# Attention with a soft mixture of experts: the products with v cut by halves of the queries, the last keys on four parts of TensorE

## The chip, the cores and the metric

One core of a Trainium2 chip runs the whole program. The metric is the device time in microseconds of one execution; three runs of the kernel before took 546.36, 547.23 and 550.35 us (median 547.23 us).

## The reference

There are 8 batches of 8 heads, 576 queries and keys, head dimension 64. What is computed, cut to what matters:

```python
scores = (q @ k.T) / 8                       # per batch and head, 576 x 576
attn = exp(scores - max) * (scores >= max - tau)
attn = attn / (sum(attn) + 1e-9)
x = attn @ v                                 # 576 x 64 per head; joined: 4608 tokens x 512
logits = x @ phi                             # 32 slots (8 experts of 4)
slots = softmax_over_tokens(logits).T @ x    # 32 x 512
slots = relu(slots @ w1[e]) @ w2[e]          # 8 experts, 512 x 1024 and 1024 x 512
out = softmax_over_slots(logits) @ slots     # 4608 x 512
```

All of it is in 32-bit floating point. The trace shows two records for each matmul on such numbers and one for each transpose.

## The kernel before

**The loop.** Two heads make a pair; the loop runs over 32 pairs (four per batch), and after each fourth pair `dispatch` (line 953) computes the logits and the running sums of that batch. In `pair` (line 717) the queries of the two heads are cut into nine blocks of 128: eight blocks of 512 "main" queries, and one block (i = 8) with the 64 left queries of both heads. For each block TensorE forms the scores (line 774; line 779 for block 8), VectorE negates them into SBUF and keeps the row maximum (L786), ScalarE takes the exponential (L796), GpSimd makes the threshold (L799), and VectorE masks and sums (L802). TensorE then transposes the masked blocks through `ptr` (line 690; 8 + 8 + 8 + 8 pieces for the main blocks, 2 for the last 64 keys of the first half, 7 for block 8 and the last keys of the second half) and ScalarE copies the transposes out of PSUM: `pTa` and `pTb` (first and second half of the queries, keys 0 to 511) and `pTl` (the 64 last keys; L695, and L874 for two pieces of 64 x 64).

**The products with v** (line 892) are two blocks of work, A (`pTa`, 256 queries) and B (`pTb`, 320 queries: 256 main and the 64 left ones). Each takes five steps over the keys (four of 128 and one of the 64 last keys) for two heads: 10 matmuls, or 20 records. Head h writes columns of the array h*64 to h*64+63, so the two heads run beside each other. The fifth step works over all 128 rows of the array, although only 64 keys are left: for head 0 rows 64 to 127 of v are zeros, for head 1 rows 0 to 63. ScalarE copies each block into `xT`; `xT` is transposed into `x`, GpSimd scales it by the reciprocal of the row sums (`ri`), and it is transposed back (line 916) and copied into `xT` (L919).

**PSUM** is four regions of two banks; each block of scores, each group of transposes and each block of products takes a region until it is copied out.

**The order of the work** is written out: `Order.add` (line 431) records each operation with its engine, a cost and its reads and writes; `TABLE` holds due times by scope (`pair0`, `pair1a`, ..., `batch`) and number; `Order.plan` (line 458) sorts each engine's queue strictly by due time and gives out buffers; `Order.run` emits the work. So the sorted due times are the order in which each engine works.

**After the loop** come the softmax over slots, the experts (`stage1`, `stage2`) and `combine`. 26 pieces of 512 KB of w1 and w2 are loaded during the loop, 20 more (`host`) into SBUF that the loop has given back, and 18 more through tiles already used; all of these loads stand in SP's queue.

**The names used below:** A, B: the two blocks of products. Scores on the array: two row halves at once (lines 774 and 690, 916), two column halves at once (line 892), four quarters at once (line 779), four column strips (lines 974, 1022, 1027: logits and running sums).

Of the kernel before, what the change touches and what calls it, by code (L numbers as in the profile page):

```python
# [17 lines left out]
LAT = {"PE": 252, "DVE": 150, "ACT": 165, "POOL": 86, "SP": 4500}  # L18
CROSS = {("PE", "DVE"): 260, ("DVE", "ACT"): 182, ("DVE", "POOL"): 220, ("ACT", "DVE"): 237, ("ACT", "POOL"): 250,
         ("POOL", "DVE"): 61, ("POOL", "ACT"): 100}  # L20
# [18 lines left out]
for _n, _v in (  # L39
    ("first", [  # L40
# [7 lines left out]
    ]),  # L48
# [8 lines left out]
    ]),  # L57
# [8 lines left out]
    ]),  # L66
# [8 lines left out]
    ]),  # L75
# [8 lines left out]
    ]),  # L84
    ("last", [
# [20 lines left out]
    ("end", [
# [29 lines left out]
    ]),  # L136
# [1260 lines left out]
```

## Time and profile before

| | |
|---|---|
| median of three runs | 547.23 us |
| profiled execution, first to last instruction (its own time) | 545.1 us |
| TensorE busy | 524.6 us, 96% |
| VectorE busy | 473.8 us, 87% |
| ScalarE busy | 459.5 us, 84% |
| GpSimd busy | 234.1 us, 43% |
| one group of four pairs, logits to logits | 57.66 us |
| granted TensorE clock, mean | 0.992 |

The loop takes about 470 of the 545 us. Busy time counts an instruction from its start to its modelled end; instructions that follow each other closely overlap, so the cost of one is better read from the distance of two starts.

### The profile page before, as it was taken

To read this page: it belongs to the slowest core of one execution; us is meant where nothing else is said; L and a number is where in the kernel's file an instruction comes from. 1 tells how busy PE (TensorE), PEld (TensorE's weight loads), DVE (VectorE), ACT (ScalarE), POOL (GpSimd) and SP (SyncE) were. 2 spreads that over 40 slices of the span, in tenths; PEclk is the share of its full clock that TensorE was granted. 3 is DMA by queue.
4 is the path that set the end of the run, shared out by engine and by line. 5 is a ranking of instruction groups with operands and counts; after the bars stand their busy time and mean duration, and the time that the engine had idled before them with its cause. 6 is when DMAs were issued, how large, how long until landed. Compare 5 with 4: busy or idle time off the path is not lost.

```text
span 545.1 us, 18237 instructions
## 1 busy us (share of the span) xinstructions
PE 524.6 (96%) x7016; PEld 339.9 (62%) x7016; DVE 473.8 (87%) x1333; ACT 459.5 (84%) x789; POOL 234.1 (43%) x475
## 2 busy tenths in 40 slices
PE   8999999999999999999999999999999999999990
PEld 6666666666666666666766666666666666644470
DVE  6999999999999999999999999998999999623192
ACT  3999998999899989999999989998999989611181
POOL 2554544554345444553455435554564445021030
PEclk9999999999999999999999999999999999999996
DMA  6433335557472738275424333333334223899598
GB/s 154 92 90 92 96 90 189 162 161 182 118 214 85 215 91 244 60 211 129 130 66 117 90 91 93 91 91 92 83 76 114 52 53 130 334 408 407 207 372 320
DMA packets 31990, 83.03 MB, mean 152 GB/s; under 512 B 4640, under 2 KB 12832, under 8 KB 31904
## 3 DMA queue, kind: packets, MB, share of 16 engines
q1 hardware_dynamic: 31584, 81.43, 49.1%
q8 instruction: 55, 0.90, 0.7%
q10 hardware_dynamic: 320, 0.44, 0.3%
q14 instruction: 31, 0.25, 0.1%
HBM read 72.42 MB, written 9.44 MB: 150 GB/s over the span
## 4 chain that ended last, share of the span: by engine, by line
PE 77%; DVE 7%; ACT 6%; DMA 4%; issue 3%; SPq 0%; DVEq 0%; POOL 0%; POOLq 0%; ACTq 0%
PE ps L892 27%; PE ps L774 22%; PE ps L690 16%; PE ps L779 3%; ACT p L796 2%; PE ps L916 2%; DVE ss L786 2%; DMA host<-in_w 2%; DMA w<-in_w 2%; DVE p L802 2%; PE ps L1022 2%; PE ps L974 2%; PE h L1219 1%; ACT pTa L695 1%; DVE host L1308 1%
## 5 line engine op out<-in xcount | busy, mean ns | idle before, releaser
L786 DVE TENSOR_SCALAR_CACHE_REDUCE ss<-ps 128x576 f32<-128x576 f32 x288 | 208.4, 752 | 12.4 <-issue 3.7
L802 DVE SCALAR_TENSOR_TENSOR p<-ss,thr,p 128x576 f32<-128x576 f32 x256 | 206.4, 836 | 2.3 <-POOL thr L799 1.4
L796 ACT ACTIVATE p<-ss,nmx 128x576 f32<-128x576 f32 x256 | 187.5, 775 | 11.0 <-DVE ss L786 10.0
L799 POOL TENSOR_SCALAR thr<-nmx,pabs 128x1 f32<-128x1 f32 x288 | 121.1, 425 | 158.4 <-DVE ss L786 148.8
L774 PE MATMUL ps<-k,q 64*128 64x288 f32 x1024 | 166.7, 429 | 0.7 <-issue 0.2
L774 PEld LDWEIGHTS ps<-k,q 64*128 64x128 f32 x1024 | 84.5, 189 | 25.9 <-ACT pTb L695 4.8
L690 PEld LDWEIGHTS ps<-ident,p 64*128 64x128 f32 x2304 | 88.9, 138 | 18.1 <-DVE ss L786 2.9
L690 PE MATMUL ps<-ident,p 64*128 64x64 f32 x2304 | 98.0, 223 | 0.4 <-ACT pTl L874 0.2
L695 ACT COPY pTb<-ps 128x1024 f32<-128x1024 f32 (+1 forms) x96 | 83.4, 877 | 2.8 <-PE ps L690 2.1
L892 PE MATMUL ps<-pTb,vv 128*64 128x320 f32 x512 | 76.0, 439 | 0.0
L695 ACT COPY pTa<-ps 128x1024 f32<-128x1024 f32 x64 | 64.9, 1015 | 1.3 <-PE ps L690 1.0
L892 PE MATMUL ps<-pTa,vv 128*64 128x256 f32 x512 | 62.3, 385 | 0.2 <-ACT pTa L695 0.2
L892 PEld LDWEIGHTS ps<-pTb,vv 128*64 128x64 f32 x512 | 33.9, 136 | 32.7 <-issue 3.9
L892 PEld LDWEIGHTS ps<-pTa,vv 128*64 128x64 f32 x512 | 33.9, 136 | 25.2 <-DVE ss L786 6.2
L911 POOL TENSOR_TENSOR x<-x,ri 128x512 f32<-128x512 f32 x31 | 34.8, 1122 | 20.0 <-ACT x L695 19.8
L892 PE MATMUL ps<-pTl,vv 128*64 128x256 f32 (+1 forms) x256 | 41.9, 406 | 0.0
L833 POOL TENSOR_SCALAR pL<-pL,ri 128x576 f32<-128x576 f32 x31 | 24.4, 788 | 27.4 <-DVE ri L829 14.5
L695 ACT COPY xT<-ps 128x256 f32<-128x256 f32 (+1 forms) x62 | 24.7, 401 | 5.3 <-PE ps L892 3.5
L802 DVE SCALAR_TENSOR_TENSOR pL<-ss,thr,pL 128x576 f32<-128x576 f32 x32 | 26.1, 816 | 1.5 <-ACT pL L796 1.4
L892 PEld LDWEIGHTS ps<-pTl,vv 128*64 128x64 f32 x256 | 18.4, 137 | 12.7
L695 ACT COPY pTl<-ps 128x256 f32<-128x256 f32 x64 | 23.9, 374 | 2.5 <-PE ps L690 1.8
L754 POOL TENSOR_SCALAR k<-k,flag 128x576 f32<-128x576 f32 x31 | 24.7, 797 | 2.9 <-DMA k<-in_kT 1.7
(166 smaller groups left out, 532.3 us busy)
## 6 DMA issues: line engine op xcount, KB each, us to landing
w<-in_w SPq DMA_DIRECT2D x44, 512.0 KB, 8.4
q<-in_qT SPq DMA_DIRECT2D x62, 288.0 KB, 4.5
vv<-in_vt SPq DMA_DIRECT2D x32, 320.0 KB, 4.2
host<-in_w SPq DMA_DIRECT2D x20, 512.0 KB, 8.5
k<-in_kT SPq DMA_DIRECT2D x62, 144.0 KB, 3.4
out<-w SPq DMA_DIRECT2D x8, 512.0 KB, 3.4
out<-host SPq DMA_DIRECT2D x8, 512.0 KB, 5.1
out<-host SPq DMA_DIRECT2D x4, 256.0 KB, 4.5
```

The source lines that it names most:

```text
L690: nc.tensor.transpose(out=s[:, g, c:c + 64], in_=ins[g], identity=ident[rows[g], rows[g]], tile_position=(64 * g, 0))
L695: G.add("ACT", 51 + 0.833 * n, nom, lambda: nc.scalar.copy(*io()), r, w)
L754: sc = lambda e, kc=kc: lambda: e.tensor_scalar(out=kt.t[:, kc], in0=kt.t[:, kc], scalar1=flag8, **one)
L774: nc.tensor.matmul(s.t[:, g, 0:HS], qt.t[rows[g], h, c * 128:(c + 1) * 128], kt.t[rows[g], h * HS:(h + 1) * HS], start=True, stop=True, ti ...
L779: nc.tensor.matmul(s.t[rows[a], g, 0:HS], qt.t[rows[g], a, SM:S], kt.t[rows[g], a * HS:(a + 1) * HS], start=True, stop=True, tile_position ...
L786: dve(674, t + OFF['mx'], [s], [ss, nmx], lambda s=s, ss=ss, nmx=nmx: nc.vector.tensor_scalar(out=ss.t.rearrange("p (a k) -> p a k", a=2), ...
L796: G.add("ACT", 668, t + OFF['ex'], lambda sv=sv, nmx=nmx, view=view: nc.scalar.activation(view().rearrange("p (a k) -> p a k", a=2), sv(), ...
L799: pool(250, t + OFF['th'], lambda nmx=nmx, thr=thr: nc.gpsimd.tensor_scalar(out=thr.t, in0=nmx.t, scalar1=1.0, scalar2=pabs, op0=ALU.mult, ...
L802: fn=lambda sv=sv, thr=thr, view=view, i=i: nc.vector.scalar_tensor_tensor(out=view().rearrange("p (a k) -> p a k", a=2), in0=sv(), scalar ...
L833: pool(725, t + OFF['sc'], lambda k=k, view=view_: nc.gpsimd.tensor_scalar(out=view(), in0=view(), scalar1=ri.t[:, k:k + 1], **one), [ri[c ...
L892: nc.tensor.matmul(lone(w)[h * 64:(h + 1) * 64, 0:n], vv.t[:, v0:v0 + 64], p0, start=(kb == 0), stop=(kb == 4), tile_position=(0, h * 64), ...
L911: G.add("POOL", 1040, u + 6.8, own=f"new{j}" + group(b), r=[ri[0]], w=[x[j]], fn=lambda: nc.gpsimd.tensor_tensor(out=wide(), in0=wide(), i ...
```

## The change

1. **Products.** For the first 31 pairs the blocks A and B now hold 256 main queries each, and the two column halves of the array take the two halves of these queries (128 each) instead of the two heads; the heads lie in the two banks of the region. A and B have 16 matmuls of 128 columns each (four steps over the keys, two heads, two halves).
2. **The last 64 keys** of A and B become work of their own, KA and KB: four matmuls of 128 columns on the four quarters of the array (rows by head, columns by half of the queries), added to the sums of A and B.
3. **The left queries** become a block L: 10 matmuls of 64 columns, two heads beside each other as before.
4. **Copies.** `pTl` takes one more third in the copy of block 8 (384 columns) instead of two copies of 64 x 64 (L874). The results are copied as 256, 256 and 64 columns instead of 256 and 320. `pL` gets a border of zeros on both sides, set once before the loop by two memsets on VectorE.
5. **Smaller work.** The reciprocals of a pair (L829, L840) and their GpSimd forerunners (L826, L837) become one each for all nine columns. The maximum of the logits is taken by the operation that also writes them negated to `l4`, so ScalarE's copy of 192 columns goes.
6. **All due times of the loop are new**, those of most pairs apart from each other, and the planner's costs of entering and leaving an arrangement of the array with them. Two of the steps of the softmax over slots (`soft`) are due later than before.
7. The last pair keeps A and B as they were, but its last keys use 64 rows.

TensorE's queue from one batch's logits to the next, sorted by due time (s0 to s8: scores; t0 to t3, tl, pT8: transposes; x, x2: transposes of the result and back; wx, w1: running sums; the number behind the point is the pair). Before, 82 pieces:

```
logits xl s2.14 A.13 dT l4 pT8.13 s0.14 wx w1 t2.13 s7.14 t3.13 s6.14 s8.14 x.12 s5.14 s4.14 t0.14 B.13 x2.12
tl.14 t1.14 s0.15 s1.15 s3.15 t2.14 s2.15 A.14 pT8.14 s6.15 t3.14 s8.15 s4.15 x.13 t0.15 s5.15 s7.15 B.14 x2.13
tl.15 t1.15 s5.16 t2.15 s1.16 s0.16 s3.16 pT8.15 t3.15 s8.16 A.15 s2.16 x.14 s6.16 s7.16 s4.16 t0.16 B.15 x2.14
tl.16 t1.16 s1.17 t2.16 s5.17 s3.17 s0.17 pT8.16 s2.17 A.16 t3.16 s7.17 x.15 s8.17 s6.17 t0.17 s3.18 B.16 s4.17
x2.15 s1.18 t1.17 tl.17
```

After, 94 pieces:

```
logits KA.13 A.13 l4 dT t2.13 s7.14 s0.14 pT8.13 wx w1 t3.13 x.12 s6.14 s4.14 s5.14 t0.14 s8.14 KB.13 L.13 B.13
tl.14 x2.12 t1.14 s0.15 s1.15 s3.15 s6.15 s2.15 t2.14 KA.14 A.14 x.13 pT8.14 s4.15 t3.14 s8.15 KB.14 t0.15 s5.15 s7.15
L.14 B.14 x2.13 t1.15 tl.15 s5.16 t2.15 s1.16 s0.16 s3.16 t3.15 pT8.15 s8.16 KA.15 A.15 x.14 s2.16 s4.16 s6.16 s7.16
t0.16 B.15 L.15 KB.15 x2.14 tl.16 t1.16 s1.17 t2.16 s0.17 s2.17 s3.17 s5.17 s6.17 t3.16 KA.16 A.16 x.15 pT8.16 s7.17
s3.18 t0.17 L.16 B.16 KB.16 s8.17 tl.17 x2.15 s4.17 s2.18 s1.18 t1.17 xl
```

The core of the diff:

```diff
+                            for a in range(2):
+                                nc.tensor.matmul(
+                                    area(w, h, l)[rows[a]], vv.t[:, (h * 4 + kb) * 64:][:, 0:64],
+                                    pT.t[:, h, kb, a * 128:(a + 1) * 128], tile_position=(0, a * 64),
+                                    **flags(w, h, a, l, 5))
+                G.add("PE", 1722, n0, main, [pTa if l == 0 else pTb[2], pTa if l == 0 else pTb[3], vv],
+                      [ab[l]["m", l], xT["t"]], mode=COLS, more=-89)
...
+            def left_keys_product(ls):
+                for l in ls:
+                    for h in range(2):
+                        for a in range(2):
+                            nc.tensor.matmul(
+                                area(ab[l], h, l)[rows[a]], vv.t[rows[h], SM + h * 64:][:, 0:64],
+                                pTl.t[rows[h], (l * 2 + a) * 128:][:, 0:128], tile_position=(64 * h, 64 * a),
+                                **flags(ab[l], h, a, l, 5))
...
                 for kb in range(5):
                     for h in range(2):
-                        v0, p0 = ((h * 4 + kb) * 64, pT.t[:, h, kb, :]) if kb < 4 else (SM + h * 64, pTl.t[:, q])
+                        v0, p0 = ((h * 4 + kb) * 64, pTb.t[:, h, kb, SM - QA:]) if kb < 4 else (
+                            SM + h * 64, pTl.t[:, SM + h * 64:][:, 0:64])
...
+                    G.add("ACT", 264, n0 + OFF['ae'], lambda l=l: nc.scalar.copy(
+                        xT.t[:, l * 256:(l + 1) * 256].rearrange("p (h x) -> p h x", h=2), ab[l].t[:, :, 0:128]),
...
-                for g in range(2):
-                    f = lambda e, w=w, g=g: e(pTl.t[rows[g], SM:S], w.t[rows[1 - g], g, 256:320])
...
+                    act_copy(384, t + OFF['te'], [w], [pTl[2]], lambda w=w: (
+                        pTl.t[:, 256:640].rearrange("p (k g q) -> p k g q", k=3, g=2),
+                        w.t[:, :, 256:448].rearrange("p g (k q) -> p k g q", k=3)))
...
+                dve(90, t + OFF['ri'], [], [ri], lambda: nc.vector.reciprocal(ri.t, ri.t))
...
-        act_copy(192, u + 1.7, [wl], [l4], lambda: (l4.t, lone(wl)[:, 0:192]))
+        G.skip(1)
```

## Rows read from the trace of the kernel before

**Rows 1.** The page, parts 1 and 4: busy time, and the chain by engine.
```profile
PE 524.6 (96%) x7016; PEld 339.9 (62%) x7016; DVE 473.8 (87%) x1333; ACT 459.5 (84%) x789; POOL 234.1 (43%) x475
...
PE 77%; DVE 7%; ACT 6%; DMA 4%; issue 3%; SPq 0%; DVEq 0%; POOL 0%; POOLq 0%; ACTq 0%
```

**Rows 2.** Chain of waits in order of time (start us, us, what), loop and tail.
```profile
2.44 3.77 DMA k<-in_kT
...
202.68 1.46 PE ps L974 x64
...
260.34 1.46 PE ps L974 x64
...
479.34 10.35 DMA host<-in_w
```

**Rows 3.** Busy time by stretches: one group of four pairs, and the loop's end.
```profile
202.68:260.34 57.66, 57.30 (x822) 38.07 (x826) 55.19 (x158) 54.84 (x95) 27.40 (x57) 1.00 0.57 159
440.00:465.00 25.00, 24.15 (x332) 15.21 (x330) 24.28 (x63) 22.97 (x39) 11.68 (x19) 1.00 0.23 77
```

**Rows 4.** TensorE's timeline (start us, us, line, tiles, forms, records), middle of the loop.
```profile
162.85 0.71 PE L774 MATMUL ps<-k,q 64*128 64x288 f32 x4
163.48 1.95 PE L892 MATMUL ps<-pTa,vv 128*64 128x256 f32 x16
...
165.79 0.52 PE L690 MATMUL ps<-ident,pL 64*128 64x64 f32 x10
...
166.28 0.70 PE L774 MATMUL ps<-k,q 64*128 64x288 f32 x4
166.82 0.65 PE L690 MATMUL ps<-ident,p 64*128 64x64 f32 x16
167.83 0.72 PE L779 MATMUL ps<-k,q 64*64 64x288 f32 x8 [0.36 <-ACT pTl L874]
168.48 0.76 PE L774 MATMUL ps<-k,q 64*128 64x288 f32 x4
169.07 0.41 PE L690 MATMUL ps<-ident,xT 64*128 64x64 f32 x8
169.31 0.67 PE L690 MATMUL ps<-ident,p 64*128 64x64 f32 x16
169.81 1.24 PE L774 MATMUL ps<-k,q 64*128 64x288 f32 x8
170.98 2.38 PE L892 MATMUL ps<-pTb,vv 128*64 128x320 f32 x16
...
173.83 0.47 PE L916 MATMUL ps<-ident,x 64*128 64x64 f32 x8
174.13 0.79 PE L690 MATMUL ps<-ident,p 64*128 64x64 f32 x20
```

**Rows 5.** Groups of weight loads: line, form, count, busy us, mean ns, idle before.
```profile
L892 PEld LDWEIGHTS ps<-pTa,vv 128*64 128x64 f32 x512 | 33.9, 136 | 25.2 <-DVE ss L786 6.2 <-ACT p L796 2.3 <-DVE ri L840 1.5
```

**Rows 6.** Groups of VectorE and ScalarE by form: the small work that changes.
```profile
L840 DVE RECIPROCAL ri<-ri 128x8 f32<-128x8 f32 x31 | 6.1, 196 | 0.0
L829 DVE RECIPROCAL ri<-ri 128x1 f32<-128x1 f32 x31 | 4.8, 156 | 1.0 <-POOL ri L826 1.0
...
L695 ACT COPY pTl<-ps 128x256 f32<-128x256 f32 x64 | 23.9, 374 | 2.5 <-PE ps L690 1.8
...
L695 ACT COPY xT<-ps 128x320 f32<-128x320 f32 x31 | 13.2, 426 | 4.1 <-PE ps L892 2.6
L874 ACT COPY pTl<-ps 64x64 f32<-64x64 f32 x62 | 12.8, 207 | 1.0
L695 ACT COPY xT<-ps 128x256 f32<-128x256 f32 x31 | 11.6, 376 | 1.2 <-PE ps L892 0.9
...
L695 ACT COPY l<-ps 128x192 f32<-128x192 f32 x8 | 2.5, 312 | 3.8 <-DVE M L980 3.8
```

**Rows 7.** Waits of SP's queue after 440 us: who, for whom, us, times, longest.
```profile
SPq L672 <- DVE p L802: 11.7, 1, 11.7
```

More of the change, by code (lines that the diff above doesn't have):

```diff
@@ L25 @@
 )
-HALVES, COLS, COLS4, QUADS, WHOLE = range(5)
-SWITCH = 145
+TURN, SCORE, QUADS, COLS, COLS4, WHOLE = range(6)
+ENTER = [
+    [0, 61, 166, 176, 0, 57],
+    [-5, 5, 166, 176, 0, 57],
+    [50, 109, 5, 176, 0, 57],
+    [50, 109, 166, 27, 0, 57],
+    [50, 109, 166, 176, 0, 57],
+    [50, 109, 166, 176, 0, 0],
+]
+LEAVE = [
+    [0, 0, 95, 95, 95, 145],
+    [0, 0, 94, 94, 94, 94],
+    [0, 0, 0, 0, 0, 0],
+    [0, 0, 0, 0, 0, 0],
+    [0, 0, 0, 0, 0, 0],
+    [94, 94, 94, 94, 94, 0],
+]
 PERIOD = 14142.5
 REGIONS = 4
+ONE = False
+QL = ((0,), (1,))
 NPRE = 26
@@ new lines @@
+    ("half0@72", [
+        18564.3, 19183.7, 19171.6, 21768.6, 24815.1,
+    ]),
+    ("half0@108", [
+        17619.3, 18238.7, 18226.6, 20823.6, 23870.1,
+    ]),
+    ("half0@144", [
+        16674.3, 17293.7, 17281.6, 19878.6, 22925.1,
+    ]),
+    ("half0@180", [
+        15729.3, 16348.7, 16336.6, 18933.6, 21980.1,
+    ]),
+    ("new0@36", [
+        36255.1, 38300.4, 43829.8,
+    ]),
+    ("new0@72", [
+        35332.1, 37355.4, 42884.8,
+    ]),
+    ("new0@108", [
+        34387.1, 36410.4, 41939.8,
+    ]),
@@ new lines @@
+    ("new0@144", [
+        33442.1, 35465.4, 40994.8,
+    ]),
+    ("new0@180", [
+        32497.1, 34520.4, 40049.8,
+    ]),
[8 rows of a table added]
+    ]),
[8 rows of a table added]
+    ]),
[8 rows of a table added]
+    ]),
[8 rows of a table added]
+    ]),
[8 rows of a table added]
+    ]),
+    ("half1@45", [
+        11263, 22477, 22477.1, 19848.3, 29943.4,
+    ]),
+    ("half1@81", [
+        10318, 21532, 21532.1, 18432, 28998.4,
+    ]),
+    ("half1@117", [
+        9373, 20587, 20587.1, 17487, 28053.4,
+    ]),
+    ("half1@153", [
+        8428, 19642, 19642.1, 16542, 27108.4,
+    ]),
+    ("half1@189", [
+        7483, 18697, 18697.1, 15597, 26163.4,
+    ]),
@@ new lines @@
+    ("new1@45", [
+        35496.9, 38263.2, 42245.1,
+    ]),
+    ("new1@81", [
+        34551.9, 37318.2, 41300.1,
+    ]),
+    ("new1@117", [
+        33606.9, 36373.2, 40355.1,
+    ]),
+    ("new1@153", [
+        32661.9, 35428.2, 39410.1,
+    ]),
+    ("new1@189", [
+        31716.9, 34483.2, 38465.1,
+    ]),
[8 rows of a table added]
+    ]),
[8 rows of a table added]
+    ]),
[8 rows of a table added]
+    ]),
[8 rows of a table added]
+    ]),
[8 rows of a table added]
+    ]),
+    ("half2@54", [
+        15249.8, 17118, 21254.7, 20558.2, 27906.7,
+    ]),
+    ("half2@90", [
+        14304.8, 16173, 20309.7, 19613.2, 26961.7,
+    ]),
@@ new lines @@
+    ("half2@126", [
+        13359.8, 15228, 19364.7, 18668.2, 26016.7,
+    ]),
+    ("half2@162", [
+        12414.8, 14283, 18419.7, 17723.2, 25071.7,
+    ]),
+    ("half2@198", [
+        11469.8, 13338, 17474.7, 16778.2, 24126.7,
+    ]),
+    ("new2@54", [
+        37182.3, 42104, 42243.2,
+    ]),
+    ("new2@90", [
+        36237.3, 41159, 41298.2,
+    ]),
+    ("new2@126", [
+        35292.3, 40214, 40353.2,
+    ]),
+    ("new2@162", [
+        34347.3, 39269, 39408.2,
+    ]),
+    ("new2@198", [
+        34882.3, 38324, 38463.2,
+    ]),
[8 rows of a table added]
+    ]),
[8 rows of a table added]
+    ]),
[8 rows of a table added]
+    ]),
[8 rows of a table added]
+    ]),
[8 rows of a table added]
+    ]),
@@ new lines @@
+    ("half3@63", [
+        19464.1, 27455.4, 26953.5, 19875.3, 26369.8,
+    ]),
+    ("half3@99", [
+        18519.1, 26510.4, 26008.5, 18930.3, 25424.8,
+    ]),
+    ("half3@135", [
+        17574.1, 25565.4, 25063.5, 17985.3, 24479.8,
+    ]),
+    ("half3@171", [
+        16629.1, 24620.4, 24118.5, 17040.3, 23534.8,
+    ]),
+    ("half3@207", [
+        15684.1, 23675.4, 23173.5, 16095.3, 22637.8,
+    ]),
+    ("new3@63", [
+        38409.6, 34233.9, 40379.2,
+    ]),
+    ("new3@99", [
+        37464.6, 33288.9, 39434.2,
+    ]),
@@ new lines @@
+    ("half0y", [
+        13990.9, 16049.9, 16050, 14094.7, 22549.3,
+    ]),
+    ("new0y", [
+        32635.1, 35748.2, 39946.9,
+    ]),
[8 rows of a table added]
+    ]),
+    ("half1y", [
+        6639.8, 10493, 12524.6, 14626.9, 25651.2,
+    ]),
+    ("new1y", [
+        32220.4, 35256.8, 38692.3,
+    ]),
[8 rows of a table added]
+    ]),
+    ("half2y", [
+        13650.3, 20747.9, 20747.8, 16505.8, 24283.6,
+    ]),
+    ("new2y", [
+        37335.5, 29638.8, 38562.9,
+    ]),
[8 rows of a table added]
+    ]),
+    ("half3y", [
+        13457.5, 15496.3, 15496.4, 18022.2, 25600.2,
+    ]),
@@ new lines @@
+    ("load0", [
+        44172.3,
+    ]),
+    ("load1", [
+        44762.3,
+    ]),
+    ("load2", [
+        31209.8,
+    ]),
+    ("load3", [
+        31799.8,
+    ]),
+    ("load4", [
+        19047.3,
+    ]),
+    ("load5", [
+        39317.3,
+    ]),
+    ("load6", [
+        31064.8,
+    ]),
+    ("load7", [
+        37662.8,
+    ]),
+    ("load8", [
+        27067.3,
+    ]),
+    ("load9", [
+        42979.3,
+    ]),
+    ("load10", [
+        29426.8,
+    ]),
+    ("load11", [
+        30816.8,
+    ]),
@@ new lines @@
+    ("load12", [
+        17264.3,
+    ]),
+    ("load13", [
+        38372.3,
+    ]),
+    ("load14", [
+        30119.8,
+    ]),
+    ("load15", [
+        36717.8,
+    ]),
+    ("load16", [
+        26122.3,
+    ]),
+    ("load17", [
+        42034.3,
+    ]),
+    ("load18", [
+        28481.8,
+    ]),
+    ("load19", [
+        29871.8,
+    ]),
+    ("load20", [
+        16319.3,
+    ]),
+    ("load21", [
+        37427.3,
+    ]),
+    ("load22", [
+        29174.8,
+    ]),
+    ("load23", [
+        35772.8,
+    ]),
@@ L392, in __init__ @@
         self.subs = {}
+        self.begun = set()
+        self.count = {}
     def __getitem__(self, k):
@@ L429, in skip, with add @@
         self.where[2] += n
-    def add(self, eng, dur, nom, fn, r=(), w=(), after=(), mode=HALVES, more=0, port=False, own=None):
+    def add(self, eng, dur, nom, fn, r=(), w=(), after=(), mode=TURN, more=0, port=False, own=None, pre=0):
         i = len(self.ops)
@@ L881, in pair @@
-        u = t0 + N9
-        for a, (pT, q) in enumerate(((pTa, slice(0, QA)), (pTb, slice(QA, S)))):
-            n0 = u + OFF['a1' if a else 'a0']
-            w = bank_of(p == NP - 1)
-            n = q.stop - q.start
-            rl = [pTl[0]] if a == 0 else [pTl[2], pTl["L", 0], pTl["L", 1]]
-            def mm(w=w, n=n, q=q, pT=pT):
+                for g in range(2 if late else 0):
+                    dve(136, t + OFF['te'], [w], [pTl["L", g]], lambda w=w, g=g: nc.vector.tensor_copy(
+                        pTl.t[rows[g], SM:S], w.t[rows[g], g, 384:448]))
@@ L905, in pair @@
-        copy(late, 512, u + OFF['xe'], [w], [x[j]], lambda w=w: (
-            x.t[:, :, j * 128:(j + 1) * 128].rearrange("p c (g d) -> p g c d", g=2),
-            w.t[:, :, 0:256].rearrange("p g (c d) -> p g c d", c=4)))
+                            lq.t[h * 64:(h + 1) * 64, 0, 256:256 + SL], vv.t[:, v0:][:, 0:64], p0,
+                            tile_position=(0, h * 64), **flags(lq, 0, h, "l", 5))
+            for ls in QL:
+                G.add("PE", 213 * len(ls), n0 + 1, lambda ls=ls: left_keys_product(ls), [vv] + [pTl[2 * l] for l in ls],
+                      [ab[l]["q", l] for l in ls], mode=QUADS, more=-68, **own)
@@ new lines, in pair @@
+            G.add("ACT", 104, n0 + OFF['ae'] + .1, lambda: nc.scalar.copy(xT.t[:, SM:S], ab[1].t[:, 0, 256:256 + SL]),
+                  [ab[1]], [xT["l"]], **own)
+            w = Buf("s")
+            ptr(4, u + OFF['x'], [xT["m", 0], xT["m", 1]], [w, x["t", j]], lambda w=w: [
+                (w.t, (l * 2 + h) * 64, [xT.t[a, xq(h, l)] for a in rows]) for l in range(2) for h in range(2)])
+            act_copy(512, u + OFF['xe'], [w], [x[j]], lambda w=w: (
+                x.t[:, :, j * 128:(j + 1) * 128].rearrange("p (l a) e -> p a l e", a=2),
+                w.t[:, :, 0:256].rearrange("p a (l e) -> p a l e", l=2)))
@@ L918, in pair @@
                 for c in range(4) for g in range(2)])
-            G.add("ACT", 477, u + 7.3, own=f"new{j}" + group(b), r=[w], w=[xT[0], xT[1]], fn=lambda w=w: nc.scalar.copy(
+            G.add("ACT", 477, u + 7.3, own=f"new{j}" + group(b), r=[w], w=[xT["m", 0], xT["m", 1]], fn=lambda w=w: nc.scalar.copy(
                 xT.t[:, 0:SM].rearrange("p (c g q) -> p g c q", c=4, g=2),
@@ L977, in dispatch @@
         for ks in ((range(HP),) if b < B - 1 else (range(2), range(2, 3), range(3, HP))):
-            G.add("PE", 1313 * len(ks) / HP, u + 1, lambda ks=ks: logits(ks), [xT[k] for k in ks] + [ph], [wl], mode=COLS4)
+            G.add("PE", 1458 * len(ks) / HP, u + 1, lambda ks=ks: logits(ks), [xT[k] for k in ks] + [ph], [wl], mode=COLS4, more=-68)
         new = batch_state(b + 1)["M"]
-        dve(269, u + 1.3, [wl], [M["own"]] if b else [new["run"]], lambda: nc.vector.tensor_reduce(
-            out=M.t[:, 0:1] if b else new.t[:, 1:2], in_=lone(wl)[:, 0:192], axis=AX.X, op=ALU.max, negate=True))
+        dve(279, u + 1.3, [wl], [M["own"] if b else new["run"], l4], lambda: nc.vector.tensor_scalar(
+            out=l4.t, in0=lone(wl)[:, 0:192], scalar1=-1.0, scalar2=3.4028234663852886e38, op0=ALU.mult, op1=ALU.min,
+            accum_out=M.t[:, 0:1] if b else new.t[:, 1:2]))
         if b > 0:
@@ L1130, in softmax_attention_soft_moe @@
         kinds[k][n] = G.slots[k][n] = sides[-1].tile(*shapes[k], name=f"{k}{n}")
+    for t in kinds["pL"]:
+        nc.vector.memset(t[:, 0:SL], 0.0)
+        nc.vector.memset(t[:, SL + S:], 0.0)
     for t in kinds["xl"]:
```

476 lines of the change are left out of this document (229 added, 247 removed), and 385 rows, old and new, of the table TABLE.

## The prediction

> **What bounds the kernel now.** I read the page first: TensorE is busy for 96% of the span and holds 77% of the chain that ends last [rows 1]. A busy TensorE need not be a full one, so I went on to the loop alone. The chain in order of time passes the logits at 202.68 and at 260.34 us [rows 2]: a group of four pairs takes 57.66 us. Busy time in just this stretch is 57.30 us for TensorE, 55.19 for VectorE and 54.84 for ScalarE [rows 3]. So TensorE misses 0.36 us in a group; VectorE and ScalarE have 2.5 and 2.8 us left. The loop goes at the pace of what TensorE's queue costs, and the next limit stands 4% below.
>
> So the question is what the new queue costs. Its order is known, as due times alone set it, and the prices stand in TensorE's timeline, where I read the distance from one start to the next, not the duration, because records overlap. The granted clock in that stretch is 1.00, the 2.4 GHz level [rows 3], so a price holds throughout.
>
> **Prices [rows 4].** A (20 records of 256 columns) takes 165.79 - 163.48 = 2.31 us, B (320 columns) 173.83 - 170.98 = 2.85. The 10 matmuls have 64 columns more in B, so 640 columns cost 0.53 us, 0.833 ns a column with two halves side by side. A streams 2560 x 0.833 = 2.13 us, so **entering** the column halves costs 0.18. The same column on four quarters costs half: line 779 has 1152 columns, 0.48 us, and takes 0.65, so entering the quarters costs 0.17. A block of scores takes 0.54 before transposes but 0.63 before A, so **leaving** for another arrangement costs 0.09. Scores take 0.48 for 576 columns, so the 0.54 holds 0.06 for coming from transposes; after line 779 they take 0.59, 0.11 for entering. Eight transposes take 0.24 after scores and 0.30 after B, 0.06 for entering; sixteen take 0.50.
>
> **The change on TensorE, one group of four pairs.**
> - The products with v in column halves: before 4 x (2.13 + 2.67) = 19.20 us. After, A and B are 16 matmuls of 128 columns, 1.71 us each, and L is 640 columns, 0.53: 4 x (1.71 + 1.71 + 0.53) = 15.80. That is **-3.40**.
> - KA and KB: 512 columns on quarters, 0.213 us each, eight of them: **+1.70**. So the last keys cost half of what they did.
> - Arrangements, counted in the two queues: the quarters are entered 8 times instead of 4 from another arrangement, +4 x 0.17 = **+0.68**; column halves 8 times in both; transposes or scores are left for another arrangement 10 times instead of 13, **-0.27**.
> - The new order puts more scores behind scores: from transposes to scores 12 times instead of 18, -0.36; scores after products or quarters never instead of 4 times, -0.44; transposes after either 10 times instead of 9, +0.06. **-0.74**.
>
> The sum is -2.03 us: 57.30 becomes 55.27. (Summed in the same way, the old queue gives 57.3, what the busy row shows.)
>
> Three kinds of step occur that the trace never shows: from L to B or back (4 in a group), from quarters to quarters (4), and from column halves to quarters (2). I bound the first two between 0 and the price of a full entry, 0.18 and 0.17, together 0 to 1.4 us; I take 0, since inside A weights and target change at every matmul and the column price leaves nothing over for it. The third I took at 0.17; its ends are 0 and 0.26, with the leaving. Short records may also be held up by their weight loads: 16 transposes, each with a load of its own, show 31 ns a record [rows 4], where KA and L need 26.7; at 31 the 36 such records of a pair cost 0.15 us more, 0.6 in a group. I take 0, the logits' 64 records in 1.46 us being the nearest short products [rows 2], and keep 0.6. So TensorE's cost lies between 54.9 and 57.5 us, and I take 55.3.
>
> **The other engines, one group.** ScalarE [rows 6]: two copies of 0.207 go and the 256-column copy grows by 128, +0.10 (64 columns more cost 0.05 between the copies of 256 and 320); 0.376 + 0.426 become 2 x 0.376 + 0.207 for the 64 columns. Per pair -0.41 + 0.10 + 0.16 = -0.15, per group -0.6, and the 192-column copy goes, -0.3: 54.84 becomes 53.9. VectorE: reciprocals of 0.156 and 0.196 become one of about 0.2, -0.6 in a group: 55.19 becomes 54.6. Taking the maximum by the other operation on the same 192 columns I put at 0 (within 0.1 either way). GpSimd is busy 27.4 of 57.66 us and loses one short operation a pair: nothing, its slack hides it; without it VectorE would wait on the threshold. The two memsets stand on VectorE ahead of the loop, while the first keys are in flight until 6.2 us [rows 2]: nothing; uncovered, some 0.2 us. The loads keep their number, and loop loads due later delay nobody, as their data is used after the loop.
>
> **What is late next.** The new period cannot go under 55.3, and VectorE then has only 0.7 us left in a group and ScalarE 1.4, instead of 2.5 and 2.8. Scores must be taken out of their PSUM region by VectorE, transposes by ScalarE, before TensorE gets the region again, so each small misfit now reaches TensorE. One misfit goes: the wait of 0.36 us before line 779, for a 64 x 64 copy, in the group before [rows 4]. I take 0.65 us of waits in a group, nearly twice today's, with ends 0.2 and 2.5: the period is about 55.95, so **-1.7** a group.
>
> **The sum.** From the logits of the first batch to those of the seventh lie six groups: -10.2 us. The first four pairs are partly paced by the first loads and by single chains; of about -0.9 on TensorE I take -0.5. At the end VectorE paces the work (24.28 of 25 us busy, [rows 3]); there the two reciprocals of each pair and the later softmax steps count, and I take -1.0 of about -1.9. The tail is a stream of weight loads; its fourth `host` load waits 11.7 us for a mask step of VectorE near the loop's end [rows 7], and TensorE then waits 10.35 us for DMA [rows 2]. So the tail hangs on the loop's end and moves with it: 0, within 2 us either way. Together -11.7: the profiled 545.1 becomes 533.4. The median of the runs lies 2.1 above that span (547.23), so I forecast **535.5 us**.
>
> **Rivals.**
> 1. *VectorE takes over.* If it keeps its 2.5 us of idle time in a group, because these come from dependencies and not from waiting on a slow TensorE, the period is 54.6 + 2.5 = 57.1 and the gain 0.6 a group, with the ends some 4.5 us: 542.7. For it: VectorE is 96% busy and no order of short, dependent steps is without holes. Against: it waits for TensorE's scores and copies today, and a quicker TensorE gives them sooner. Chance 0.17.
> 2. *Slower: weight loads pace the halved products.* There are 100 records with their own load in a pair's products instead of 40, and a load of 64 columns lasts 136 ns on average [rows 5]. If loads go one after another at L ns each, the 36 records that need 26.7 ns cost 36 x (L - 26.7). The gain is about 0.5 us a pair, so this decides from L = 41 ns. At half of 136, 68 ns, the 64 records of A and B (53 ns each) suffer too: +2.4 us a pair, near 605 us in all; at 50 ns +0.84 a pair, a net +0.34 over 31 pairs: 558. Against: transposes run at 31 ns with 128-column loads [rows 4], and the logits at 23 [rows 2]. Chance 0.06. The Trainium skill, TensorE: Matmul & The Clock Gate, LDWEIGHTS, prices a load at its columns over 1.2, 53 ns here, an estimate by which the kernel would take some 561 us; the transposes contradict it, at 31 ns where it says 107.
> 3. *PSUM regions run short.* KB sometimes begins before other work (in pair 14 a group of transposes and two scores stand between it and L), so the region of B stays taken some 2 us longer while only four exist. At 0.5 us of stall a pair the gain is gone (547); twice that gives 562. Against: before, too, four regions sufficed at 0.36 us lost. Chance 0.07 together, half of it within 1%.
> 4. *The change does not do what it says:* the two queues above show that it does; no chance of its own.
>
> **How the numbers follow.** The forecast has 0.70. Its own range comes from the unseen steps and the waits: 55.3 + 0.2 gives -13.5 and with the ends and a tail 2 us better about 529; 56.2 + 0.8 gives -4 and with the ends 541. Rival 1 has 0.17, rivals 2 and 3 0.13. A range of **529 to 545** takes in rival 1 and leaves the slower ones and a little below out, under 2 in 10. One per cent is 5.5 us, about what a measurement tells from no change: faster than 541.8 are nearly all of the forecast and a third of rival 1, 0.74; within 1% the rest of rival 1 and half of rival 3, 0.16; slower 0.10.
>
> **What will show it.** In the profile after: a period between logits of 55.5 to 56.5 us; A and B at about 1.9 us with their entry, KA and KB near 0.21 behind other quarters; no L874 on ScalarE; VectorE and ScalarE at 97% and 96% of a group. The forecast is wrong in its price if A and B run well over 1.9 us, or L to B shows a gap near 0.18; wrong in its waits if TensorE idles over 1.5 us a group, and then the row's releaser (VectorE or ScalarE) says which rival it is.

## The result, and the profile after

The changed kernel takes **539.59 us** (median, 537.61 to 540.20), the kernel before in the same job 546.96 (546.36 to 550.35): a ratio of 0.985, 95% interval 0.981 to 0.988. It is 1.5% faster, inside the range, and 4.1 us above the forecast. The profiled execution has a span of 537.6 us against 545.1.

The page, parts 1 and 4, beside [rows 1]. ScalarE and VectorE have less work, as counted; TensorE stays at 96% of a shorter span. The share of DMA in the chain goes from 4% to 8%.
```profile
PE 515.4 (96%) x8876; PEld 403.2 (75%) x8876; DVE 468.8 (87%) x1312; ACT 445.0 (83%) x750; POOL 229.8 (43%) x444
...
PE 73%; DMA 8%; DVE 7%; ACT 5%; issue 3%; POOL 1%; SPq 1%; DVEq 0%; POOLq 0%
```
Part of that is a late load of v, shown below; most of the rest is the end, where two `host` loads of weights stand in the chain one behind the other, and before only one did [rows 2]:
```profile
460.63 10.06 DMA host<-in_w
470.75 10.21 DMA host<-in_w
```

The logits mark the groups, as in [rows 2]. TensorE's timeline, the logits of the second to fourth batch:
```profile
141.66 1.53 PE L1352 MATMUL ps<-xT,phi_sb 128*32 128x128 f32 x64
...
201.36 1.53 PE L1352 MATMUL ps<-xT,phi_sb 128*32 128x128 f32 x64
...
257.70 1.51 PE L1352 MATMUL ps<-xT,phi_sb 128*32 128x128 f32 x62
```
All such starts, and the distance from one to the next (us). Before, the eighth logits come in two parts, and the start is that of the first:

| | 1st logits | groups 1 to 6 | 7th to 8th logits | 8th to end |
|---|---|---|---|---|
| before | 87.25 | 57.68 57.68 57.66 57.69 57.73 57.68 | 36.17 | 75.6 |
| after | 85.38 | 56.28 **59.70** 56.34 56.48 56.69 56.74 | 37.07 | 72.9 |

So five groups gain 0.9 to 1.4 us each (5.9 in all), the second **loses** 2.0, the head (the time up to the first logits) gains 1.9 and everything behind the seventh logits 1.7: 5.9 - 2.0 + 1.9 + 1.7 = 7.5 us.

Busy time of a regular group and of the loop's end (columns as in [rows 3]). TensorE's own busy time went from 57.30 to 56.17, not to 55.3; it now misses 0.17 us of the group instead of 0.36. VectorE stands at 96%, ScalarE at 94%. At the loop's end TensorE has no gap left (the stretch is the same by the clock, so it lies 5.8 us further on in the work than before).
```profile
201.36:257.70 56.34, 56.17 (x1062) 46.60 (x1058) 54.34 (x155) 52.88 (x91) 26.53 (x52) 1.00 0.58 163
440.00:465.00 25.00, 24.97 (x428) 18.79 (x426) 21.44 (x59) 22.07 (x38) 9.77 (x15) 1.00 0.55 204
```

TensorE's timeline in that group, beside [rows 4]. Read the starts. Scores of block 8 and KB, both on quarters, take 212.87 - 212.01 = 0.86 us together, which is 0.65 + 0.21 by the prediction's prices, so a step from quarters to quarters costs nothing. KA behind the logits takes 0.38 and A behind it 1.89, 0.17 and 0.18 over their columns. L and B together take 215.35 - 212.87 = 2.48; their columns and one entry make 2.42, so the step from L to B costs 0.06 to 0.07. The scores at 209.86 wait 0.17 us for a ScalarE copy; four of the groups show such a wait, up to 0.3 us.
```profile
202.82 0.45 PE L1249 MATMUL ps<-pTl,vv 64*64 64x128 f32 x8
203.20 1.97 PE L1237 MATMUL ps<-pTa,vv 128*64 128x128 f32 x32
205.09 0.34 PE L1010 MATMUL ps<-ident,l 64*128 64x64 f32 x4
...
209.86 1.73 PE L1094 MATMUL ps<-k,q 64*128 64x288 f32 x12 [0.17 <-ACT pTb L1015]
...
212.01 0.71 PE L1099 MATMUL ps<-k,q 64*64 64x288 f32 x8
212.54 0.40 PE L1249 MATMUL ps<-pTl,vv 64*64 64x128 f32 x8
212.87 0.69 PE L1260 MATMUL ps<-pTb,vv 128*64 128x64 f32 x16
213.39 0.29 PE L1260 MATMUL ps<-pTl,vv 128*64 128x64 f32 x4
213.50 1.92 PE L1237 MATMUL ps<-pTb,vv 128*64 128x128 f32 x32
215.35 0.34 PE L1010 MATMUL ps<-ident,p 64*128 64x64 f32 x4
```

The weight loads of the products, beside [rows 5], and the small work, beside [rows 6]:
```profile
L1237 PEld LDWEIGHTS ps<-pTa,vv 128*64 128x64 f32 x992 | 53.5, 137 | 5.5 <-issue 4.3 <-ACT pTa L1015 0.5 <-DVE ss L1106 0.4
...
L1275 ACT COPY xT<-ps 128x256 f32<-128x256 f32 x62 | 23.2, 375 | 7.5 <-PE ps L1237 3.5 <-PE ps L1249 2.9
L1278 ACT COPY xT<-ps 128x64 f32<-128x64 f32 x31 | 6.7, 215 | 0.6 <-PE ps L1249 0.6
L1147 DVE RECIPROCAL ri<-ri 128x9 f32<-128x9 f32 x31 | 6.5, 208 | 0.0
```

Now the bad group. The chain of waits in order of time, 140 to 180 us: TensorE stands for 1.06 us, in the middle of block L, with no releaser named, and later the chain leaves it altogether, for SyncE's queue and a load of v.
```profile
153.86 1.06 issue
...
169.43 0.76 SPq L990
170.19 0.05 issue
170.25 6.84 DMA vv<-in_vt
177.09 0.14 issue
177.23 0.45 PE ps L1249 x8
```
SyncE's queue at that place (start, time, line, what, times). The load of v for pair 11 stands behind that of k for pair 13, which waits for its buffer until 168.04, and behind a load of weights. TensorE is free for KA of pair 11 at 175.7, 5.5 us after the issue, and gets v at 177.2.
```profile
154.65 1.24 SPq L1072 DMA_DIRECT2D q<-in_qT  x2
168.04 1.34 SPq L1058 DMA_DIRECT2D k<-in_kT  x2
169.43 0.76 SPq L990 DMA_DIRECT2D w<-in_w  x1
170.25 0.90 SPq L1079 DMA_DIRECT2D vv<-in_vt  x2
```
In the kernel before, the queue has the same order at this place, and there are no more than 5.2 us from the issue to the use:
```profile
173.14 0.59 SPq L670 DMA_DIRECT2D w<-in_w  x1
173.78 0.90 SPq L759 DMA_DIRECT2D vv<-in_vt  x2
...
178.97 1.95 PE L892 MATMUL ps<-pTa,vv 128*64 128x256 f32 x16
```
What differs is the landing. The two loads of v issued there landed after 4.1 and 6.1 us before, and after 6.8 and 8.2 in the changed kernel (smallest, median and largest of the two):
```profile
DMA to landing us min/median/max: 4.1/5.1/6.1
DMA to landing us min/median/max: 6.8/7.5/8.2
```
A wait of SyncE's queue behind 440 us, beside [rows 7]: there a `host` load waited 11.7 us for a mask step, and now one waits 10.9 us for the loop's last scores of block 8.
```profile
SPq L992 <- PE ps L1099: 10.9, 1, 10.9
```

### The profile page after: what moved, and what is told of

The parts are those of the page before. It is cut to its first block, busy times and chain, and to the rows that moved or that the text cites. A ratio compares the mean times of both kernels' runs of the same rounds, so it can differ in the third digit from the quotient of the medians.

```text
span 537.6 us, 21853 instructions
## 1 busy us (share of the span) xinstructions
PE 515.4 (96%) x8876; PEld 403.2 (75%) x8876; DVE 468.8 (87%) x1312; ACT 445.0 (83%) x750; POOL 229.8 (43%) x444
## 4 chain that ended last, share of the span: by engine, by line
PE 73%; DMA 8%; DVE 7%; ACT 5%; issue 3%; POOL 1%; SPq 1%; DVEq 0%; POOLq 0%
PE ps L1094 21%; PE ps L1237 19%; PE ps L1010 16%; DMA host<-in_w 4%; PE ps L1260 4%; PE ps L1249 3%; PE ps L1099 3%; DVE ss L1106 3%; DMA w<-in_w 2%; ACT p L1116 2%; PE ps L1294 2%; DVE p L1122 2%; PE h L1602 1%; ACT pTa L1015 1%; DMA vv<-in_vt 1%
## 5 line engine op out<-in xcount | busy, mean ns | idle before, releaser
L1119 POOL TENSOR_SCALAR thr<-nmx,pabs 128x1 f32<-128x1 f32 x288 | 128.4, 452 | 144.8 <-DVE ss L1106 141.3
L1094 PE MATMUL ps<-k,q 64*128 64x288 f32 x1024 | 154.0, 421 | 1.9 <-ACT pTb L1015 0.9
L1237 PE MATMUL ps<-pTa,vv 128*64 128x128 f32 x992 | 61.0, 276 | 0.1
L1237 PE MATMUL ps<-pTb,vv 128*64 128x128 f32 x992 | 60.1, 274 | 0.0
L1237 PEld LDWEIGHTS ps<-pTa,vv 128*64 128x64 f32 x992 | 53.5, 137 | 5.5 <-issue 4.3
L1237 PEld LDWEIGHTS ps<-pTb,vv 128*64 128x64 f32 x992 | 53.7, 137 | 2.1 <-issue 1.0
L1145 POOL TENSOR_SCALAR ri<-r 128x9 f32<-128x9 f32 x31 | 6.2, 200 | 55.5 <-DVE p L1122 51.4
L1275 ACT COPY xT<-ps 128x256 f32<-128x256 f32 x62 | 23.2, 375 | 7.5 <-PE ps L1237 3.5
L1249 PE MATMUL ps<-pTl,vv 64*64 64x128 f32 x496 | 26.9, 287 | 1.5 <-DMA vv<-in_vt 1.5
L1559 POOL TENSOR_TENSOR c<-lall,crow 128x512 f32<-128x512 f32 x9 | 9.3, 1044 | 37.5 <-PE ct L1002 22.3
```

The source lines that it names most:

```text
L1094: nc.tensor.matmul(s.t[:, g, 0:HS], qt.t[rows[g], h, c * 128:(c + 1) * 128], kt.t[rows[g], h * HS:(h + 1) * HS], start=True, stop=True, ti ...
L1119: pool(250, t + OFF['th'], pre=75, fn=lambda nmx=nmx, thr=thr: nc.gpsimd.tensor_scalar(out=thr.t, in0=nmx.t, scalar1=1.0, scalar2=pabs, op ...
L1237: nc.tensor.matmul(area(w, h, l)[rows[a]], vv.t[:, (h * 4 + kb) * 64:][:, 0:64], pT.t[:, h, kb, a * 128:(a + 1) * 128], tile_position=(0, ...
L1249: nc.tensor.matmul(area(ab[l], h, l)[rows[a]], vv.t[rows[h], SM + h * 64:][:, 0:64], pTl.t[rows[h], (l * 2 + a) * 128:][:, 0:128], tile_po ...
L1275: G.add("ACT", 264, n0 + OFF['ae'], lambda l=l: nc.scalar.copy(xT.t[:, l * 256:(l + 1) * 256].rearrange("p (h x) -> p h x", h=2), ab[l].t[ ...
```

## The experiments

**The two parts apart.** `products_alone` has the new products, with the due times of the kernel before and its two reciprocals (what stands in angle brackets is shortened); `order_alone` the old products in the new order.
```diff
 # products_alone: the changed code
-TABLE.update(<the new due times>)
+TABLE.update(<the due times before; KA, KB, L beside A and B>)
 # order_alone: the code before
-TABLE.update(<the due times before>)
+TABLE.update(<the new due times>)
```


> The new products (halves of the queries, last keys on four quarters, merged copies) in the old order: KA stands behind A, L and KB behind B, and the reciprocals are the old two. Theory T (TensorE's queue sets the pace): per group of four pairs -3.40 us for the products, +1.70 for KA and KB, +1.33 for eight entries into the quarters and +0.26 for four steps from B to L, so TensorE's cost is 57.2 us, as before (57.3): 545 to 549 us in all, the same as the kernel before. Rival V (the gain comes from the work taken off ScalarE and VectorE): as ScalarE loses 0.6 us a group here too, at least half of the gain stays, under 543 us.

Measured 547.38 us, ratio 1.000 (0.999 to 1.001), groups of 57.2 to 57.4 us: as the theory had it. By its sum, the new products in the old order give back, in changes of arrangement and in KA and KB, nearly all that they save. ScalarE has less work here too and nothing is gained by that, so rival V is out.

> The old products and copies in the new order (A at the place of KA and A, B at the place of L or KB, the old reciprocals and copies beside their successors). Theory T: fewer changes between scores, transposes and products, TensorE's cost 56.3 us a group against 57.3; with 0.8 us of waits, 57.1 against 57.67, so 541 to 545 us. Rival V: without the lighter ScalarE and VectorE the new order gains nothing, 546 us or more.

Measured **558.78** us, ratio 1.022 (1.019 to 1.024): a miss. Its first four groups take 57.3 to 57.5 us, but the fifth and sixth 61.7 and 61.3, and the first logits start at 90.8. TensorE's waits behind 370 us show what breaks: the copies out of PSUM come late. The order was laid out for other products, and I take that to be why.
```profile
PE ps L668 <- ACT pTb L471: 2.5, 2, 2.1
PE ps L466 <- ACT l L471: 2.0, 2, 1.7
```
So neither part gains alone with the due times as they are; the gain needs both.

**The last keys.** `keys_on_halves` runs KA and KB with the same columns on column halves, all 128 rows, instead of quarters.
```diff
 # shortened
-vv.t[rows[h], SM + h * 64:][:, 0:64], pTl.t[rows[h], (l * 2 + a) * 128:][:, 0:128], tile_position=(64 * h, 64 * a)
+vv.t[:, SM + h * 64:][:, 0:64],       pTl.t[:, (l * 2 + a) * 128:][:, 0:128],       tile_position=(0, 64 * a)
```
It contracts over 128 rows where 64 hold the last keys.

> The changed kernel with one edit: KA and KB work on the two column halves over all 128 rows, as the fifth step did before, in the same places of the queue. Theory T: eight times 0.213 us more a group, less the entries into the quarters that go; summed piece by piece TensorE's cost rises by 1.6 us a group, of which waits give back up to 0.4: 9 to 13 us slower than the changed kernel, 548 to 553 us. Rival V (another engine sets the pace, TensorE has slack): under 3 us slower, 540 to 543 us.

Measured 547.09 us, ratio 0.999 (0.997 to 1.001), 7.5 us slower than the changed kernel, where 9 to 13 were expected: the mechanism holds, the size is some 1.5 us under. Its third to sixth groups take 57.5 to 57.8 us, 0.9 to 1.1 longer than in the changed kernel; the first two take 58.8 and 58.7, with a wait of 1.5 us for v in the first and a stop of 0.8 us without a releaser in the second. Without the quarters nothing is left of the gain.

**The late v.** `weights_spread` loads the 26 weight tiles of the loop one per pair, from the fourth pair on, instead of two per pair.
```diff
-G.scope(f"load{i}", (i // 2 + 3) * N9)
-G.add("SP", 590, (i // 2 + 3) * N9, lambda i=i: load_unit(wslots[i]), after=[qload[i // 2 + 3]])
+G.scope(f"wl{i}", (i + 3) * N9)
+G.add("SP", 590, (i + 3) * N9 + 5, lambda i=i: load_unit(wslots[i]), after=[qload[i + 3]])
```


> The changed kernel with the 26 weight loads of the loop one to a pair from the fourth pair on, not two to a pair from the fourth to the sixteenth; the queues of the four compute engines keep their order. Theory D (the second group of the changed kernel took 59.7 us instead of 56.4 because the load of v for pair 13 landed late behind weight loads, 6.8 us instead of 4.7): that group falls to about 56.5 and the time by 2 to 3 us, to 537. Rival: the group was long because TensorE's instructions came late (1.06 us without a releaser), which the loads of weights don't change: under 1 us.

(The late load is that of pair 11; 13 is the pair of the load of k ahead of it.) Measured 537.01 us, ratio 0.982 (0.980 to 0.984). The second group is cured (56.47), but the fourth is now 58.57, with the same picture in its chain, pair 19 for pair 11:
```profile
281.77 0.58 SPq L990
282.40 7.40 DMA vv<-in_vt
```
So I put the load of v itself first. `v_first` changes nothing but four places in SyncE's queue, for pairs 7, 11, 15 and 19:
```diff
+TABLE.update({(f"pair3@{9 * p}", 4): TABLE[f"pair1@{9 * (p + 2)}", 0] + 2 * PERIOD - 1 for p in (7, 11, 15, 19)})
```


> The changed kernel, with four loads of v (pairs 7, 11, 15 and 19) put ahead of one load of k in SyncE's queue; no other queue differs. Theory: the second group is 59.70 us against 56.3 to 56.7 because v of pair 11 stands behind k of pair 13, which waits for its buffer until 168.04, and then lands at 177 while the product wants it at 175.7. Then the second group comes to 56.2-56.8 and the whole to 536-537.5 us. Rival A: the 1.06 us in which TensorE issues nothing at 153.86 belongs to that group for another reason and stays: second group 57.3-57.8, the whole 537.5-538.7. Rival B: v now waits in the queue for its own buffer and holds k back, the scores wait: 539.5 or more, with waits of the scores on k.

Measured 536.75 us, ratio 0.979 (0.976 to 0.981). No wait on v is left, the second group falls from 59.70 to 57.87, the others stay as they were (56.06 to 56.77). The total stands where the theory put it, but the group where rival A did, just above its upper edge of 57.8: 1.8 us were the late v, and the stop of 1.06 us without a releaser is another thing and stays. TensorE's waits in the loop:
```profile
PE ps L1260 <- issue: 1.1, 1, 1.1
PE ps L1094 <- ACT pTb L1015: 0.9, 4, 0.3
...
```
`v_first_spread` is `v_first` with the weights spread as above.

> The same four loads of v first, and the 26 loop loads of weights one per pair as in weights_spread (there 537.01 us with the fourth group at 58.57 us and a load of v of 7.40 us in its chain). Theory: both lateness cases are one and the same queue, so all six groups come to 56.0-56.8 us, the whole to 534.5-535.7 us. Rival: one late group turns up again wherever the transfers are crowded, since the landing time and not the order decides: one group above 58 us and the whole at 536.5-537.5 us.

Measured 536.63 us, ratio 0.980 (0.978 to 0.982). All six groups take 56.08 to 56.67 us, and the stop is gone too; but the total misses, as the first logits come at 86.82 instead of 85.38. `v_first_late` therefore starts the weights at the sixth pair (`i + 5` for `i + 3`).

> The changed kernel with four loads of v first (as in v_first) and the 26 loop loads of weights one per pair, but from the sixth pair on instead of the fourth. In v_first_spread all six groups came to 56.1-56.7 us, yet the first logits started at 86.82 us instead of 85.38. Theory: that 1.4 us is the price of the weights that now load beside the first pairs' own loads. Then the first logits come back to 85.0-85.6 us with the six groups as they were: 534.5-535.8 us, the best of all versions. Rival: the head is late for another reason (the order of SyncE's queue), the first logits stay at 86.3 us or later: 536-537 us. Second rival: a late group returns, since weights now load until the loop's last pairs: above 537 us.

Measured **536.44** us, ratio 0.979 (0.977 to 0.981). The first logits are back at 85.56, five groups at 56.09 to 56.67; the sixth takes 57.12. Weights load there, but in `v_first_spread` they do so too, where it takes 56.43, so they alone are not the reason; TensorE waits 0.4 us for a threshold of GpSimd there, and why was not tried. The theory of the head holds, the total is 0.6 us above what was expected, and against `v_first` (0.3 us) nothing is gained that can be measured. Either one is faster than both kernels.

What the stop is: the DMA traffic of the single microsecond from 152 us, in the changed kernel, shows one packet of an instruction load among 88 data packets that fill 92% of the 16 engines' time:
```profile
q1 hardware_dynamic: 88, 0.32, 92.3%
q8 instruction: 1, 0.02, 6.9%
```
In `v_first_spread` one instruction packet is all that moves from 152 to 155 us, and TensorE runs through:
```profile
q14 instruction: 1, 0.01, 1.3%
```
That fits TensorE waiting for instructions held up by loads of weights. Two more runs bear on it. In `scalar_light` (below) the packet comes a microsecond later, at 153 to 154 us, and TensorE stops in the same block L, at 155.4 for 0.5 us. `vector_light` has its weights as the changed kernel has them and no stop; there an instruction packet moves at 149 to 150 us, three microseconds earlier, though the engines are just as full (103%). So it would be the time of the instruction load that counts, and spreading the weights is one way to move it. No run delays an instruction load by itself, so it is argued, not shown.

**What is left in a regular group.** Is the rest above 55.3 us waiting, or TensorE's own work? `vector_light` masks only half of the columns of blocks 7 and 8 (blocks of queries, though the expectations call them key blocks) in pairs 2 to 23, `scalar_light` does so with the exponential, `both_light` does both on top of `v_first_late`.
```diff
 # vector_light, shortened (scalar_light: the same slice in the exponential)
-in0=sv(), scalar=thr.t, in1=view()...
+in0=sv()[:, :, c2], scalar=thr.t, in1=view()...[:, :, c2]   # c2 = slice(0, HS // 2 if i >= 7 and 2 <= p < 24 else HS)
```


> The changed kernel, but in pairs 2 to 23 the masking of key blocks 7 and 8 by VectorE covers half of the columns (the rest of these two blocks keeps its unmasked values); nothing else differs. VectorE loses an estimated 0.3-0.4 us per instruction, some 2.4-3.2 us of its 54 us per group. TensorE's own work by its prices is 55.3-55.6 us per group, the measured periods are 56.3-56.7. Theory V (the 0.8-1.2 us left over per group are waits that VectorE causes, 96% busy in the loop): groups 3 to 6 fall to 55.6-56.0, the whole to 536-537.3 us (its late second group stays). Theory N (they come from elsewhere): groups 3 to 6 within 0.15 us of 56.3-56.7, the whole 539-540 us.

> The changed kernel, but in pairs 2 to 23 the exponential of key blocks 7 and 8 by ScalarE covers half of the columns (the rest of these two blocks keeps old values); nothing else differs. ScalarE loses an estimated 0.25-0.35 us per instruction, some 2-2.8 us of its 53 us per group. Theory S (the 0.8-1.2 us left over per group beside TensorE's own work come from ScalarE's copies and exponentials being late): groups 3 to 6 fall to 55.6-56.0, the whole to 536-537.3 us. Theory V or N (VectorE, or neither): groups 3 to 6 within 0.15 us of 56.3-56.7, the whole 539-540 us. If both light kernels gain, the two engines share the chain from a score to its probabilities and each shortens it.

> The kernel v_first_late, but in pairs 2 to 23 both the exponential and the masking of key blocks 7 and 8 cover half of the columns (the rest of the two blocks keeps old or unmasked values), so that VectorE is busy some 2 us and ScalarE some 2 us less per group. vector_light alone took 0.3 us per group from groups 3 to 6 (56.05-56.40 instead of 56.34-56.74), scalar_light alone 0-0.3. TensorE's own work by its prices is 55.3 us per group, 55.55 with the 0.07 us measured for each step between L and B. Theory N (what is left above 55.55 is TensorE's own: prices slightly too low, steps unseen before): groups 3 to 6 stay at 56.0-56.4 us. Theory E (the engines together still hold it back): groups 3 to 6 come to 55.5-55.9 us.

Measured: `vector_light` 536.70 us, 0.980 (0.977 to 0.983); `scalar_light` 539.54, 0.985 (0.982 to 0.988); `both_light` 533.72, 0.975 (0.973 to 0.978). The totals also hold whether v came late (in `scalar_light` twice, 3.3 us in all; in `vector_light` once, 0.6) and the stop, so I read the fourth group. Its busy time in the changed kernel, `vector_light`, `scalar_light` and `both_light`, in this order:
```profile
257.70:314.18 56.48, 56.19 (x1063) 46.59 (x1059) 54.47 (x155) 52.90 (x91) 27.08 (x52) 1.00 0.36 98
```
```profile
254.47:310.61 56.14, 56.12 (x1062) 46.41 (x1058) 52.54 (x155) 52.83 (x91) 25.97 (x52) 1.00 0.37 99
```
```profile
260.25:316.68 56.43, 56.12 (x1062) 46.33 (x1059) 54.48 (x155) 51.36 (x91) 27.15 (x52) 1.00 0.38 99
```
```profile
253.56:309.76 56.20, 56.18 (x1062) 46.55 (x1058) 52.47 (x155) 51.35 (x91) 26.03 (x52) 1.00 0.46 127
```
Take 1.9 us from VectorE, and TensorE's gap, the first number less the second, falls from 0.29 to 0.02; take 1.5 from ScalarE, and it stays at 0.31; take both, and it is 0.02 again. So VectorE costs 0.3 us a group, neither theory V's 0.8 nor nothing; the visible wait for ScalarE's copy is VectorE's too, since it goes when VectorE gets lighter.

TensorE's busy time, the second number, stands at 56.12 to 56.19 in all four, and the period of `both_light` lies where theory N put it. But that does not make the 0.6 us above 55.55 TensorE's own work, because busy time hides short waits: a record of scores counts as busy for 0.40 us, to an end that is modelled, and two start every 0.24 us. Look at the runs of scores in the chain, the first from the kernel before, the others from `both_light`:
```profile
233.61 1.51 PE ps L774 x12
...
282.82 1.65 PE ps L1094 x12
295.96 2.60 PE ps L1094 x20
307.58 1.51 PE ps L1094 x12
```
Twelve records cost 1.51 before and in one run of `both_light`, but 1.65 in the other. Twenty would cost 2.48 (0.54 for four and 0.485 for each four more), and take 2.60. In the run of 1.65 us, the record that begins the second block of scores waits for a semaphore, and by the time of the semaphore it is ScalarE's copy of `pTa` that lets it go. The copy ends at 282.16 + 1.02 = 283.18, and the record starts at 283.23:
```profile
282.16 1.02 ACT L1015 COPY pTa<-ps 128x1024 f32<-128x1024 f32 x1
283.23 0.51 PE L1094 MATMUL ps<-k,q 64*128 64x288 f32 x2
```
The fourth group of `both_light` has four such places, each starting 0.05 to 0.07 us behind the end of what it waits for: two copies of `pTa` (0.14 and 0.12 us lost), a copy of `pTb` (0.23) and VectorE's work on a block of scores (0.10), 0.6 us in all. The same four stand in the third and fourth groups of the changed kernel, where with the visible idle time they make 0.75 and 0.86 us. So what lies above 55.55 is mostly waiting for PSUM regions, as theory E had it; its period did not come because the light kernels leave these waits. This is read from the traces; no run takes the four waits away.

## Why the prediction was right or wrong

**Right.** The sign, the range and the forecast's mechanism: a regular group gets shorter because TensorE's queue costs less. A and B at 1.9 us, KB at 0.21 behind other quarters and no step between quarters came as announced. VectorE's estimate of 54.6 us a group measured 54.3 to 54.5, ScalarE's 53.9 measured 52.9. Rival 2 is out: 20 records of L and 32 of B, each with its own weight load, run at the price of their columns, 2.48 us with one entry and one step. By the Trainium skill, TensorE: Matmul & The Clock Gate, LDWEIGHTS, a load of 64 columns takes 53 ns, an estimate of 2.8 us for these 52 if one load followed the other. The 2.48 us show that they do not. Rival 3 is out as well. It asked for 0.5 us a pair on the region of B; the regions that TensorE waits for in a regular group are those of the copies of `pTa` and `pTb` and of one block of scores, at about 0.2 us a pair. Rival 1, VectorE taking over at 57.1 us, is out with 0.3 us a group.

**Wrong in size: TensorE's queue, "-2.03 us: 57.30 becomes 55.27".** The busy rows say 56.12 to 56.19, but 0.6 of that is the short waits in the runs of scores. Without them the queue costs about 55.6, a step of -1.7. Of the 0.3 us that are missing, 4 x 0.065 = 0.26 is the step from L to B, taken at 0 with 0.18 as the other end. The products were not mis-sized by much: `products_alone` came out at its 57.2 us, with L to B at 0.07. The price of scores held too: a run of 12 costs 1.51 us before, and after where it need not wait.

**Nearly right: the waits, "I take 0.65 us".** The idle row shows 0.2 to 0.3 in a regular group, but with those that busy time hides the third and fourth groups have 0.75 and 0.86. Both terms were taken too small: the periods are 56.3 to 56.7 instead of 55.95, and a group gains 0.9 to 1.4 us instead of 1.7. Over the five regular groups that is 5.9 us instead of 8.5.

**Failed: "The loads keep their number, and loop loads due later delay nobody, as their data is used after the loop."** I asked who waits for the moved loads, and not who stands behind them. In SyncE's queue the load of v for every fourth pair stands behind a load of k that waits for its buffer, and then beside weights, with little more than 5 us to its use. It stood there before as well, and landed in time. In all five kernels with the new products in the new order and the loads of v at their old place (the changed one, `keys_on_halves`, `weights_spread`, `vector_light`, `scalar_light`) TensorE waits for v once or twice in the loop, 0.6 to 3.3 us in all; in the kernel before, `products_alone` and `order_alone` never. What makes the landing longer is open. It cost 1.8 us in the second group (`v_first`), and the stop of 1.06 us stands beside it; 0.3 of the 3.2 us by which that group exceeds the regular ones I can't place.

**The ends.** The head gave -1.9 instead of -0.5; since `products_alone` starts its first logits at 87.92 and `order_alone` at 90.8, only both together bring it, and why was not tried. Behind the seventh logits -1.7 came instead of -1.0 plus 0. The last products with v end earlier, so the loads of weights that wait for them go out 3.8 us closer to the seventh logits (37.2 instead of 41.0 us), and the first products of the tail start 3.0 us closer (53.4 instead of 56.4 us). The tail gives 1.2 back, 0.8 of it before a load of weights that takes 10.93 us instead of 10.11.

Sum: six groups -3.9 (predicted -10.2), head -1.9 (-0.5), end and tail -1.7 (-1.0): -7.5 instead of -11.7. One slip in the prediction's own sum changes nothing here: a period of 55.3 + 0.2 gives six times 2.16, or -13.0 us, where it says -13.5.

## What to carry to other kernels

When the order of an engine's work changes, look in the load queues for what stands *behind* a load that waits for its buffer: four places in one queue took 1.8 us out of one group here, and the kernel before had the same queue without paying for it. Do not take a busy share near 100% for an engine that never waits: where ends are modelled, compare the starts of like runs (1.51 and 1.65 us here) and see what each longer one waited for. A part that gains nothing alone, like these products (1.000) or this order (1.022), may still be what makes the other one pay.

## What was not expected of the hardware

- TensorE can stand for 1.06 us in the middle of a row of matmuls with nothing to wait for that the profile shows, while an instruction load and full DMA engines are about. With the weights spread this is gone, and in `vector_light` without.
- The same load of v (320 KB), at the same place of the queue behind loads of k and weights, landed in 4.1 us before, in 6.8 in the changed kernel and in 4.2, 5.3 and 6.4 in `keys_on_halves`, `vector_light` and `scalar_light` (one execution each). So standing behind a load of weights does not by itself make it late.
- A wait of 0.1 to 0.2 us between two blocks of scores leaves no gap in TensorE's busy time; it shows only as a longer distance of starts.
- Two blocks of products in the same column halves, L and B, still cost 0.06 to 0.07 us at their seam; quarters behind quarters cost nothing.
